# Three first passes with gate/up blocks kept on chip, passes that begin with resident blocks, and an early matmul order left to the scheduler

## Chip, cores and metric

One core of a Trainium2 chip. The metric is device microseconds of one execution. "Span" is the profiled execution's length, which is about 2 us shorter than its timed run.

Names used below: PE is the matmul engine, PEld its weight load, DVE the vector engine, ACT the scalar engine, POOL the GpSimd engine, SP the engine that issues most loads. "Idle" of an engine is a stretch's length less its busy time. Tile names in the texts: xn is the layer-normed input, hT and h2T its transposes for the projections and for gate/up, qT and kT the projected q and k, v_sb the v rows, vd their copy in memory, vsh the shifted v rows read back from it, prod and lgT the products of q and k and their sums, o_sb and oT the attention's output and its transpose, pgu and gu the gate and up results, wd and wo the loaded w_down and output weights, wmA to wmC parts of w_mod.

## The reference, cut

A transformer block on 2048 rows of 576 columns, bf16, with conditioning vectors from a small product `silu(c) @ w_mod`:

```python
h = layernorm(x) * (1 + ca) + sa
x = x + ga * attention(h, wqkv, wo)      # 32 heads of 18; each row sees 8 rows, every second one back
h = layernorm(x) * (1 + cb) + sb
x = x + gb * ((h @ w_gate) * (h @ w_up)) @ w_down     # 576 -> 4608 -> 576
```

## The kernel before

Rows are cut into chunks of 128, 128 and then 256. `period(ci)` emits the attention of chunk `ci` and the projections (q, k, v) of chunk `ci + 1`. A pass multiplies one group of chunks by all of w_gate and w_up, in nine blocks of 1.18 MB; after the last pass of a group, `down` multiplies its 512 rows by w_down. While pass i runs, a pacer emits the periods of the chunks of pass i+1 between its matmuls.

```python
SIZES = [128, 128, 256, 256, 256, 256, 256, 256, 256]
DOWN = [[[0], [1, 2]], [[3, 4]], [[5, 6]], [[7, 8]]]   # passes of 128, 384, 512, 512, 512 columns
FB = 4
GU_BUFS = 3                                             # ring of three block buffers
# ... cut
load_rows(nc.sync, wmB, w_mod[:, 3 * D:5 * D])
load_rows(nc.sync, wo, wod)                             # wod: A_wo reordered by way of a scratch copy in memory
# ... cut
for b in range(GU_BUFS):
    load_gu(0, b)                                       # blocks 0 to 2 before the first pass
# ... cut: in gate_up, after each block's matmuls
            if i == FB - 1:
                nb = b + GU_BUFS
                load_gu(pi + nb // (FT // FB), nb % (FT // FB))
                if pi == 0:
                    load_wd(b)                          # w_down is read during pass 0
# ... cut: the end of the kernel
    for _ in period(0):
        pass
    with tc.manual_schedule(engines={PE}):              # from here on PE runs in the order of emission
        passes = [(di, p) for di, d in enumerate(DOWN) for p in d]
        for pi, (di, p) in enumerate(passes):
            # ... cut
            step = Pacer(passes[pi + 1][1] if pi + 1 < len(passes) else [], total)
            step(0)
            gate_up(pi, home[p[0]][1], C, h2T[di], step)
            if last:
                down(r0, [t for q in DOWN[di] for c in q for t in x_tiles[c]], step)
            step(0, rest=True)
```

Outside `manual_schedule` the framework's scheduler chooses the order on each engine, by its own model of durations. The order then stands on the chip: in the trace of the kernel before, PE waits 2.9 us (to 123.2 us) for ACT's copy of the v rows, with gate/up matmuls behind that wait in its order.

Of the kernel before, what the change touches and what calls it, by code (L numbers as in the profile page):

```python
# [7 lines left out]
BF = mybir.dt.bfloat16  # L8
F32 = mybir.dt.float32
ALU = mybir.AluOpType  # L10
ACTF = mybir.ActivationFunctionType
# [5 lines left out]
P = 128  # L17
D = 576
DP = 640
KT = 5  # L20
H = 32
DH = 18
# [4 lines left out]
FT = FF // P  # L27
# [3 lines left out]
CM = 512  # L31
CH = 256
SIZES = [128, 128, 256, 256, 256, 256, 256, 256, 256]

DOWN = [[[0], [1, 2]], [[3, 4]], [[5, 6]], [[7, 8]]]
FB = 4
GU_BUFS = 3

AT = dict(lg0=.06, lg1=.14, lgT=.19, hT=.24, q0=.29, q1=.34, k0=.39, k1=.44, qkr=.48, v0=.52, v1=.57,
          oT=.66, wo0=.70, wo1=.74, h2T=.92)  # L40
# [3 lines left out]
def kernel(  # L44
# [37 lines left out]
    def att(shape, dt, name):  # L82
        return ps_att.tile(shape, dt, name=name, tag="att")
# [36 lines left out]
    kT = once.tile([P, KT, HALO + CH], BF, name="kT")  # L120
    v_sb = once.tile([P, D], BF, name="v_sb")
    vd = dramp.tile([HALO + S, D], BF, name="vd")
    wod = dramp.tile([D, D], BF, name="wod")

    nc.gpsimd.memset(wqk[64:, KT - 1, :], 0.0)
    nc.gpsimd.memset(wo[64:, KT - 1, :], 0.0)
# [13 lines left out]
    def load_rows(eng, dst, src):  # L140

        eng.dma_start(dst[:, 0:KT - 1, :], src[0:(KT - 1) * P, :].rearrange("(k p) n -> p k n", p=P))
        eng.dma_start(dst[0:64, KT - 1, :], src[(KT - 1) * P:D, :])
# [2 lines left out]

    setup_guard = tc.tile_pool(name="setup", bufs=1)
    sp = setup_guard.__enter__()
    c_bf = sp.tile([P, KT], BF, name="c_bf")
    nc.vector.memset(c_bf[:], 0.0)  # L150
    with nc.allow_non_contiguous_dma(reason="tiny column-layout load of c"):
        nc.sync.dma_start(c_bf[:, 0:KT - 1], c[0, 0:(KT - 1) * P].rearrange("(m p) -> p m", p=P))
        nc.sync.dma_start(c_bf[0:64, KT - 1:KT], c[0, (KT - 1) * P:D].rearrange("(m p) -> p m", p=64))

    def wm_tile():
        return sp.tile([P, KT, 2 * D], BF, name="wm", bufs=2)
# [12 lines left out]
    wmC = wm_tile()  # L169
    load_rows(nc.sync, wmC[:, :, 0:D], w_mod[:, 2 * D:3 * D])  # L170
    load_rows(nc.sync, wmC[:, :, D:2 * D], w_mod[:, 5 * D:6 * D])
    nc.sync.dma_start(wod[:, :].rearrange("(d h) n -> d h n", d=DH), A_wo.rearrange("(h d) n -> d h n", d=DH))
    wmB = wm_tile()
    load_rows(nc.sync, wmB, w_mod[:, 3 * D:5 * D])
    load_rows(nc.sync, wo, wod)

    c_f = sp.tile([P, KT], F32, name="c_f")
    nc.vector.tensor_copy(c_f[:], c_bf[:])
    e_f = sp.tile([P, KT], F32, name="e_f")
    nc.scalar.activation(e_f[:], c_f[:], ACTF.Exp, scale=-1.0)  # L180
    nc.vector.tensor_scalar_add(e_f[:], e_f[:], 1.0)
    nc.vector.reciprocal(e_f[:], e_f[:])
    sc = sp.tile([P, KT], BF, name="sc")
    nc.vector.tensor_tensor(sc[:], c_f[:], e_f[:], ALU.mult)
    sc_bc = sp.tile([P, KT, P], BF, name="sc_bc")
    nc.vector.tensor_copy(sc_bc[:], sc[:, :, None].to_broadcast([P, KT, P]))

# [29 lines left out]


    gu_blocks = {}

    def load_gu(mi, b):
        if mi >= sum(len(d) for d in DOWN):
            return
        gm = gwp.tile([P, KT - 1, 2, FB * P], BF, name="gm")
        gr = gwp.tile([P, 2, FB * 64], BF, name="gr")
        c0 = b * FB * P
        for t, wsrc in enumerate((B_w_gate, B_w_up)):
            nc.sync.dma_start(gm[:, :, t, :], wsrc[0:(KT - 1) * P, c0:c0 + FB * P].rearrange("(k p) n -> p k n", p=P))
            for half in range(2):
                nc.sync.dma_start(gr[64 * half:64 * (half + 1), t, :],  # L230
                                  wsrc[(KT - 1) * P:D, c0 + half * FB * 64:c0 + (half + 1) * FB * 64])
        gu_blocks[mi, b] = (gm, gr)

    def load_wd(b):
        n = FT * FB // FT
        nc.sync.dma_start(wd[:, b * n:(b + 1) * n, :], B_w_down[b * n * P:(b + 1) * n * P, :].rearrange("(k p) n -> p k n", p=P))

    for b in range(GU_BUFS):
        load_gu(0, b)

    def setup_mid():
        for t in range(2):
# [17 lines left out]
    def ln_rows(src):  # L260
        ST = len(src)
        stats = small.tile([P, CH // P, 2, 6], F32, name="ln_stats")
        mv = small.tile([P, CH // P, 2], F32, name="ln_mv")
        for j in range(ST):
            for hf in range(2):
                nc.vector.bn_stats(stats[:, j, hf, :], src[j][:, hf * 288:(hf + 1) * 288])  # L266
            nc.vector.bn_aggr(mv[:, j, :], stats[:, j, :, :].rearrange("p a b -> p (a b)"))
        rstd = small.tile([P, CH // P], F32, name="ln_rstd")
        nc.vector.tensor_scalar_add(rstd[:, 0:ST], mv[:, 0:ST, 1], EPS)
        nc.scalar.activation(rstd[:, 0:ST], rstd[:, 0:ST], ACTF.Ln)  # L270
        nc.scalar.activation(rstd[:, 0:ST], rstd[:, 0:ST], ACTF.Exp, scale=-0.5)
        nmr = small.tile([P, CH // P], F32, name="ln_nmr")
        nc.vector.scalar_tensor_tensor(nmr[:, 0:ST], mv[:, 0:ST, 0], -1.0, rstd[:, 0:ST], ALU.mult, ALU.mult)  # L273
        for j in range(ST):
            nc.scalar.activation(xn[:, j, 0:D], src[j][:], ACTF.Identity, bias=nmr[:, j:j + 1], scale=rstd[:, j:j + 1])  # L275
            nc.gpsimd.tensor_copy(xn[:, j, D:], xn[:, j, D - 64:D])

    def ln_cols(dst, C, vi, act_only=False):

# [161 lines left out]
    def gate_up(pi, c0, C, h2, step):  # L441

        hh = late["hh"]
        cs = slice(c0, c0 + C)
        ns = C / 2.4
        pss = {}
        for f in range(FT):
            b, i = f // FB, f % FB
            gm, gr = gu_blocks[pi, b]

            fi = (i // 2) + 2 * (i % 2)
            ps = ps_mlp.tile([P, 2, 512], F32, name="pgu", tag="mlp")
            pss[i % 2] = ps
            for t in range(2):
                for kt in range(KT - 1):
                    nc.tensor.matmul(ps[:, t, 0:C], lhsT=gm[:, kt, t, fi * P:(fi + 1) * P], rhs=h2[:, kt, cs],  # L456
                                     start=(kt == 0), stop=False, skip_group_check=True)
            if i % 2 == 0:
                step(8 * ns)
                continue  # L460
            for t in range(2):
                for hf in range(2):
                    rows = slice(64 * hf, 64 * (hf + 1))
                    nc.tensor.matmul(pss[hf][:, t, 0:C], lhsT=gr[rows, t, (i // 2) * P:(i // 2 + 1) * P],  # L464
                                     rhs=h2[rows, KT - 1, cs], start=False, stop=True, skip_group_check=True)
            with hp():
                for hf in range(2):
                    fo = b * FB + i // 2 + 2 * hf
                    gu = late["gup"].tile([P, 2, CM], BF, name="gu")
                    nc.scalar.copy(gu[:, :, 0:C], pss[hf][:, :, 0:C])  # L470
                    nc.vector.tensor_tensor(hh[:, fo, cs], gu[:, 0, 0:C], gu[:, 1, 0:C], ALU.mult)  # L471
            if i == FB - 1:
                nb = b + GU_BUFS
                load_gu(pi + nb // (FT // FB), nb % (FT // FB))
                if pi == 0:
                    load_wd(b)
            step(10 * ns)

    def down(r0, x_t, step):
        hh = late["hh"]  # L480
        for j in range(CM // P):
            acc = ps_mlp.tile([P, 2, 512], F32, name="acc", tag="mlp")
            for f in range(FT):
                for q in range(2):
                    nc.tensor.matmul(acc[:, q, 0:288], lhsT=hh[:, f, j * P:(j + 1) * P], rhs=wd[:, f, q * 288:(q + 1) * 288],  # L485
                                     start=(f == 0), stop=(f == FT - 1))
                step(240)
            with hp():
                o_t = late["outp"].tile([P, D], BF, name="y")
                nc.vector.tensor_tensor(o_t[:].rearrange("p (n d) -> p n d", n=2), acc[:, :, 0:288],  # L490
                                        gb_bc[:].rearrange("p (n d) -> p n d", n=2), ALU.mult)
                nc.vector.tensor_tensor(o_t[:], o_t[:], x_t[j][:], ALU.add)  # L492
            nc.gpsimd.dma_start(out_flat[r0 + j * P:r0 + (j + 1) * P, :], o_t[:])  # L493
# [50 lines left out]
    for _ in period(0):  # L544
        pass

    with tc.manual_schedule(engines={PE}):
        passes = [(di, p) for di, d in enumerate(DOWN) for p in d]
        for pi, (di, p) in enumerate(passes):
            last = p is DOWN[di][-1]  # L550
            C = sum(SIZES[c] for c in p)
            total = FT * 9 * C / 2.4 + (FT * CM // P * 240 if last else 0)
            step = Pacer(passes[pi + 1][1] if pi + 1 < len(passes) else [], total)
            step(0)
            gate_up(pi, home[p[0]][1], C, h2T[di], step)
            if last:
                r0 = START[DOWN[di][0][0]]
                down(r0, [t for q in DOWN[di] for c in q for t in x_tiles[c]], step)
            step(0, rest=True)


# [28 lines left out]
```

## Time and profile before

| | value |
|---|---|
| median of the first 3 runs | 656.75 us (656.70 to 659.48) |
| span of the profiled run | 655.4 us |
| PE busy | 586.0 us (89%) |
| moved by DMA | 92.38 MB |

From the page of the kernel before: busy time by engine, then 40 equal slices of the span (16.4 us each) with PE's busy share in tenths and PE's granted clock in tenths of full speed.

```profile
PE 586.0 (89%) x4405; PEld 347.6 (53%) x4449; DVE 311.5 (48%) x657; ACT 257.4 (39%) x432; POOL 62.7 (10%) x139
...
PE   3665858678999999999999999999999999999996
...
PEclk9965989779999999999999899999999999999999
```

PE is full from the eleventh digit on. The loss is in the ten before it, where the granted clock is lower at times as well.

The same in four stretches of the kernel before: set-up; to the start of the second pass; to the start of the first 512-column pass (just after the first down); the rest. Columns: stretch, its length, busy time and count of PE, PEld, DVE, ACT and POOL, granted PE clock, DMA share, GB/s.

```profile
core 0: us, PE busy (x) PEld busy (x) DVE busy (x) ACT busy (x) POOL busy (x), PEclk, DMA share, GB/s
0.00:58.46 58.46, 30.46 (x321) 23.06 (x323) 26.25 (x71) 17.82 (x48) 17.54 (x42) 0.82 0.90 290
58.46:141.02 82.56, 58.65 (x652) 42.49 (x656) 51.51 (x126) 36.09 (x90) 8.36 (x19) 0.85 0.69 217
141.02:269.21 128.19, 123.64 (x964) 77.80 (x967) 70.66 (x147) 55.94 (x97) 13.41 (x30) 0.97 0.46 142
269.21:655.40 386.19, 373.22 (x2473) 204.25 (x2504) 163.11 (x314) 147.59 (x199) 23.36 (x48) 1.00 0.33 102
```

The second line: PE is idle 82.56 - 58.65 = 23.9 us there, with DVE busy 51.5 us.

### The profile page before, as it was taken

The numbers are of one execution on the slowest core, as the hardware profiler recorded it, in microseconds if no ns is written. First come the engines' busy times: TensorE is split into PE (matmuls) and PEld (weight loads), VectorE is DVE, ScalarE is ACT, GpSimd is POOL, SyncE is SP. The second block draws the span as 40 slices with busy tenths as digits, with TensorE's granted clock in tenths as the row PEclk, the third lists the DMA queues.
The fourth block names the chain that finished last, engine by engine and source line by source line (L and its number), as shares of the span: only waits on it lengthen the run. The fifth ranks groups of instructions, "written<-read, shape, count | busy, mean of one in ns | idle before, by whom it ended". The sixth has DMA issues, their size and how long they took to land.

```text
span 655.4 us, 10904 instructions
## 1 busy us (share of the span) xinstructions
PE 586.0 (89%) x4405; PEld 347.6 (53%) x4449; DVE 311.5 (48%) x657; ACT 257.4 (39%) x432; POOL 62.7 (10%) x139
## 2 busy tenths in 40 slices
PE   3665858678999999999999999999999999999996
PEld 2453646334654677544443677454445773333575
DVE  2364738547545675376346635384447432222111
ACT  2333554245456411354475222354554023444300
POOL 4401010100010012200100011100000000000000
PEclk9965989779999999999999899999999999999999
DMA  8979784744376514143733331234645102542000
GB/s 277 321 265 324 221 269 145 259 122 131 122 226 190 146 63 138 37 145 109 261 110 118 109 101 56 81 109 135 210 146 144 56 10 81 145 145 72 1 19 19
DMA packets 81035, 92.38 MB, mean 141 GB/s; under 512 B 6601, under 2 KB 74265, under 8 KB 80985
## 3 DMA queue, kind: packets, MB, share of 16 engines
q1 hardware_dynamic: 72153, 65.73, 33.6%
q0 software_dynamic: 5952, 23.01, 9.9%
q10 hardware_dynamic: 2880, 2.95, 1.3%
q8 instruction: 35, 0.57, 0.3%
q14 instruction: 15, 0.12, 0.1%
HBM read 86.93 MB, written 5.40 MB: 141 GB/s over the span
## 4 chain that ended last, share of the span: by engine, by line
PE 67%; DVE 12%; DMA 8%; issue 6%; ACT 5%; SPq 1%; POOL 0%; POOLq 0%; DVEq 0%; ACTq 0%
PE pgu L456 32%; PE acc L485 15%; PE pgu L464 6%; PE pq L316 4%; DMA wm<-in_w_mod_dram 3%; PE lgT L375 2%; DVE vsh L409 2%; PE pw L429 2%; PE pv L332 2%; DMA gm<-in_B_w_up_dram 1%; DMA vsh<-vd 1%; DVE ln_stats L266 1%; ACT xn L275 1%; DMA wv_raw<-in_A_wqkv_dram 1%; ACT gu L470 1%
## 5 line engine op out<-in xcount | busy, mean ns | idle before, releaser
L456 PE MATMUL pgu<-h2T,gm 128*128 128x512 bf16 (+2 forms) x1409 | 276.8, 344 | 5.2 <-ACT h2T L292 2.3
L470 ACT CAST gu<-pgu 128x1024 bf16<-128x1024 f32 (+2 forms) x180 | 143.0, 844 | 163.5 <-PE pgu L464 156.4
L456 PEld LDWEIGHTS <-gm 128*128 128x128 bf16 x1440 | 129.3, 101 | 130.7 <-issue 28.4
L485 PE MATMUL acc<-wd,hh 128*128 128x288 bf16 x1152 | 146.1, 286 | 0.0
L471 DVE TENSOR_TENSOR hh<-gu 128x512 bf16<-128x512 bf16 (+2 forms) x180 | 65.2, 369 | 158.7 <-ACT gu L470 158.3
L485 PEld LDWEIGHTS <-hh 128*128 128x128 bf16 x1152 | 111.4, 98 | 29.6 <-issue 1.3
L366 DVE TENSOR_TENSOR prod<-qT,kT 128x1280 bf16<-128x1280 bf16 (+1 forms) x72 | 46.3, 686 | 22.1 <-PE lgT L375 21.9
L316 PE MATMUL pq<-hT,wqk 128*128 128x256 bf16 (+1 forms) x360 | 45.9, 280 | 10.4 <-DVE hT L290 6.7
L409 DVE TENSOR_TENSOR vsh<-vsh,attn 128x2304 bf16<-128x2304 bf16 x32 | 42.6, 1353 | 15.1 <-DMA vsh<-vd 15.0
L353 POOL DMA_DIRECT2D vsh<-vd x32 | 24.0, 751 | 266.5 <-DVE vsh L410 122.8
L464 PE MATMUL pgu<-h2T,gr 64*128 64x512 bf16 (+2 forms) x360 | 47.4, 343 | 0.9
L316 PEld LDWEIGHTS <-wqk 128*128 128x128 bf16 x360 | 34.3, 107 | 21.0 <-issue 15.4
L490 DVE TENSOR_TENSOR y<-acc,gb_bc 128x576 bf16<-128x576 f32 x16 | 12.1, 754 | 50.2 <-PE acc L485 50.2
L266 DVE BATCH_NORM_STATS2 ln_stats<-x_t 128x6 f32<-128x288 bf16 x64 | 25.6, 438 | 6.1 <-DMA x_t<-in_A_x_dram 5.6
L275 ACT ACTIVATE xn<-x_t,ln_nmr,ln_rstd 128x576 bf16<-128x576 bf16 x32 | 27.0, 863 | 2.2 <-DVE ln_nmr L273 1.7
L464 PEld LDWEIGHTS <-gr 64*128 64x128 bf16 x360 | 10.3, 95 | 31.0 <-issue 27.6
L493 POOL DMA_DIRECT2D out_dram<-y x16 | 8.8, 549 | 168.1 <-DVE y L492 158.1
L429 PE MATMUL pw<-wo,oT 128*128 128x512 bf16 x74 | 23.6, 413 | 0.6 <-ACT oT L422 0.6
L285 PE MATMUL ln_pA<-ident,xn 128*128 128x128 bf16 x128 | 11.0, 228 | 12.2 <-ACT xn L275 12.2
L410 DVE TENSOR_TENSOR vsh<-vsh 128x2304 bf16<-128x2304 bf16 x16 | 21.7, 1353 | 0.2
L332 PE MATMUL pv<-wv,hT 128*128 128x512 bf16 x74 | 21.2, 380 | 0.4 <-ACT kT L318 0.2
L336 ACT CAST v_sb<-pv 128x512 bf16<-128x512 f32 x16 | 9.4, 589 | 30.3 <-PE pvr L334 17.6
(98 smaller groups left out, 394.9 us busy)
## 6 DMA issues: line engine op xcount, KB each, us to landing
gm<-in_B_w_gate_dram SPq DMA_DIRECT2D x45, 512.0 KB, 3.8
gm<-in_B_w_up_dram SPq DMA_DIRECT2D x45, 512.0 KB, 4.9
vsh<-vd POOLq DMA_DIRECT2D x32, 576.0 KB, 5.5
wd<-in_B_w_down_dram SPq DMA_DIRECT2D x9, 576.0 KB, 9.9
gr<-in_B_w_gate_dram SPq DMA_DIRECT2D x90, 32.0 KB, 3.6
gr<-in_B_w_up_dram SPq DMA_DIRECT2D x90, 32.0 KB, 4.2
wm<-in_w_mod_dram SPq DMA_DIRECT2D x2, 1152.0 KB, 10.0
vd<-v_sb ACTq DMA_DIRECT2D x16, 144.0 KB, 3.9
```

Of the source, the lines that this page charges most:

```text
L266: nc.vector.bn_stats(stats[:, j, hf, :], src[j][:, hf * 288:(hf + 1) * 288])
L275: nc.scalar.activation(xn[:, j, 0:D], src[j][:], ACTF.Identity, bias=nmr[:, j:j + 1], scale=rstd[:, j:j + 1])
L316: nc.tensor.matmul(pq[:, gi, 0:C], lhsT=wqk[:, kt, w0:w0 + P], rhs=hT[:, kt, 0:C], start=(kt == 0), stop=(kt == KT - 1))
L332: nc.tensor.matmul(pv[:], lhsT=hT[:, kt, j * P:(j + 1) * P], rhs=wv[:, kt, 0:512], start=(kt == 0), stop=(kt == KT - 1))
L366: nc.vector.tensor_tensor(prod[:, 0:nm, 0:C], qT[:, 0:nm, 0:C], kT[:, 0:nm, off:off + C], ALU.mult)
L409: nc.vector.tensor_tensor(vsh[:], vsh[:], attn[:, j, ws, None, :].to_broadcast([P, WG, DH, H]), ALU.mult)
L429: nc.tensor.matmul(pw[:], lhsT=oT[:, m, j * P:(j + 1) * P], rhs=wo[:, m, 0:512], start=(m == 0), stop=(m == KT - 1))
L456: nc.tensor.matmul(ps[:, t, 0:C], lhsT=gm[:, kt, t, fi * P:(fi + 1) * P], rhs=h2[:, kt, cs], start=(kt == 0), stop=False, skip_group_check ...
L464: nc.tensor.matmul(pss[hf][:, t, 0:C], lhsT=gr[rows, t, (i // 2) * P:(i // 2 + 1) * P], rhs=h2[rows, KT - 1, cs], start=False, stop=True, ...
L470: nc.scalar.copy(gu[:, :, 0:C], pss[hf][:, :, 0:C])
L471: nc.vector.tensor_tensor(hh[:, fo, cs], gu[:, 0, 0:C], gu[:, 1, 0:C], ALU.mult)
L485: nc.tensor.matmul(acc[:, q, 0:288], lhsT=hh[:, f, j * P:(j + 1) * P], rhs=wd[:, f, q * 288:(q + 1) * 288], start=(f == 0), stop=(f == FT ...
```

## The change

The intent: more matmul work where PE has none, and freedom to use it. The first 512 rows go through gate/up in three passes (128, 128, 256) instead of two (128, 384). A third pass would read all nine blocks again, so four of them stay on chip for these passes, in the memory of w_down, which is read only when pass 2 has used them. Each pass begins with blocks that the pass before left in the ring. PE's order in these three passes is the scheduler's. Three set-up edits come along: c is loaded as rows and transposed on PE, wo is loaded by eighteen small copies without the scratch copy, and a 64-column copy moves from POOL to ACT.

```diff
-DOWN = [[[0], [1, 2]], [[3, 4]], [[5, 6]], [[7, 8]]]
+DOWN = [[[0], [1], [2]], [[3, 4]], [[5, 6]], [[7, 8]]]
+AUTO = 3
+ORDER = [[0, 1, 2, 3, 4, 5, 6, 7, 8], [6, 7, 8, 5, 4, 3, 2, 1, 0], [2, 3, 4, 5, 8, 1, 0, 6, 7],
+         [0, 6, 7, 1, 2, 3, 4, 5, 8], [4, 5, 8, 0, 1, 2, 3, 6, 7], [3, 6, 7, 0, 1, 2, 4, 5, 8]]
+KEPT = [2, 3, 4, 5]
 ...
-    c_bf = sp.tile([P, KT], BF, name="c_bf")            (c in columns)
+    c_row = sp.tile([KT, P], BF, name="c_row")          (c in rows; silu on rows; transposed on PE)
 ...
-    nc.sync.dma_start(wod[...], A_wo...)                 (ahead of wmB)
     wmB = wm_tile()
     load_rows(nc.sync, wmB, w_mod[:, 3 * D:5 * D])
-    load_rows(nc.sync, wo, wod)
+    for d in range(DH):
+        r0 = d % 4 * H
+        nc.sync.dma_start(wo[r0:r0 + H, d // 4, :], A_wo.rearrange("(h d) n -> d h n", d=DH)[d])
 ...
+    def block_done(pi, b):
+        if pi == 2 and b in KEPT:
+            k = KEPT.index(b)
+            load_wd(k * WDB, (k + 1) * WDB)
+        for n in range(len(loads)):
+            if last_use[n] == (pi, b) and n + GU_BUFS == state["next"]:
+                load_next()
+    for b in ORDER[0]:
+        if b in KEPT:
+            load_gu(b, KEPT.index(b))                     (into the memory of w_down)
+        elif state["next"] < GU_BUFS:
+            load_next()
+    load_wd(len(KEPT) * WDB, FT)
 ...
-            nc.gpsimd.tensor_copy(xn[:, j, D:], xn[:, j, D - 64:D])
+            nc.scalar.activation(xn[:, j, D:], src[j][:, D - 64:], ...)
 ...
+    for pi in range(AUTO):
+        run_pass(pi)                                      (PE order by the scheduler)
     with tc.manual_schedule(engines={PE}):
-        for pi, (di, p) in enumerate(passes):
+        for pi in range(AUTO, len(passes)):
+            run_pass(pi)
```

More of the change, by code (lines that the diff above doesn't have):

```diff
@@ L33 @@
 SIZES = [128, 128, 256, 256, 256, 256, 256, 256, 256]
-DOWN = [[[0], [1, 2]], [[3, 4]], [[5, 6]], [[7, 8]]]
+DOWN = [[[0], [1], [2]], [[3, 4]], [[5, 6]], [[7, 8]]]
 FB = 4
+AUTO = 3
 GU_BUFS = 3
+NB = FT // FB
+ORDER = [[0, 1, 2, 3, 4, 5, 6, 7, 8], [6, 7, 8, 5, 4, 3, 2, 1, 0], [2, 3, 4, 5, 8, 1, 0, 6, 7],
+         [0, 6, 7, 1, 2, 3, 4, 5, 8], [4, 5, 8, 0, 1, 2, 3, 6, 7], [3, 6, 7, 0, 1, 2, 4, 5, 8]]
+KEPT = [2, 3, 4, 5]
 AT = dict(lg0=.06, lg1=.14, lgT=.19, hT=.24, q0=.29, q1=.34, k0=.39, k1=.44, qkr=.48, v0=.52, v1=.57,
@@ L122 @@
     vd = dramp.tile([HALO + S, D], BF, name="vd")
-    wod = dramp.tile([D, D], BF, name="wod")
     nc.gpsimd.memset(wqk[64:, KT - 1, :], 0.0)
@@ L148 @@
     sp = setup_guard.__enter__()
-    c_bf = sp.tile([P, KT], BF, name="c_bf")
-    nc.vector.memset(c_bf[:], 0.0)
-    with nc.allow_non_contiguous_dma(reason="tiny column-layout load of c"):
-        nc.sync.dma_start(c_bf[:, 0:KT - 1], c[0, 0:(KT - 1) * P].rearrange("(m p) -> p m", p=P))
-        nc.sync.dma_start(c_bf[0:64, KT - 1:KT], c[0, (KT - 1) * P:D].rearrange("(m p) -> p m", p=64))
+    c_row = sp.tile([KT, P], BF, name="c_row")
+    nc.vector.memset(c_row[:], 0.0)
+    nc.sync.dma_start(c_row[0:KT - 1, :], c[0, 0:(KT - 1) * P].rearrange("(m p) -> m p", p=P))
+    nc.sync.dma_start(c_row[KT - 1:KT, 0:64], c[0:1, (KT - 1) * P:D])
     def wm_tile():
@@ L171 @@
     load_rows(nc.sync, wmC[:, :, D:2 * D], w_mod[:, 5 * D:6 * D])
-    nc.sync.dma_start(wod[:, :].rearrange("(d h) n -> d h n", d=DH), A_wo.rearrange("(h d) n -> d h n", d=DH))
     wmB = wm_tile()
     load_rows(nc.sync, wmB, w_mod[:, 3 * D:5 * D])
-    load_rows(nc.sync, wo, wod)
-    c_f = sp.tile([P, KT], F32, name="c_f")
-    nc.vector.tensor_copy(c_f[:], c_bf[:])
-    e_f = sp.tile([P, KT], F32, name="e_f")
+    for d in range(DH):
+        r0 = d % 4 * H
+        nc.sync.dma_start(wo[r0:r0 + H, d // 4, :], A_wo.rearrange("(h d) n -> d h n", d=DH)[d])
+    c_f = sp.tile([KT, P], F32, name="c_f")
+    nc.vector.tensor_copy(c_f[:], c_row[:])
+    e_f = sp.tile([KT, P], F32, name="e_f")
     nc.scalar.activation(e_f[:], c_f[:], ACTF.Exp, scale=-1.0)
@@ L182 @@
     nc.vector.reciprocal(e_f[:], e_f[:])
+    sc_row = sp.tile([KT, P], BF, name="sc_row")
+    nc.vector.tensor_tensor(sc_row[:], c_f[:], e_f[:], ALU.mult)
+    pc = att([P, KT], BF, "pc")
+    nc.tensor.transpose(pc[:], sc_row[:], ident[0:KT, 0:KT])
     sc = sp.tile([P, KT], BF, name="sc")
-    nc.vector.tensor_tensor(sc[:], c_f[:], e_f[:], ALU.mult)
+    nc.vector.tensor_copy(sc[:], pc[:])
     sc_bc = sp.tile([P, KT, P], BF, name="sc_bc")
@@ L219, with load_gu @@
     gu_blocks = {}
-    def load_gu(mi, b):
-        if mi >= sum(len(d) for d in DOWN):
-            return
-        gm = gwp.tile([P, KT - 1, 2, FB * P], BF, name="gm")
-        gr = gwp.tile([P, 2, FB * 64], BF, name="gr")
+    wd_flat = wd[:].rearrange("p f d -> p (f d)")
+    GM, GR = (KT - 1) * 2 * FB * P, 2 * FB * 64
+    def load_gu(b, kept=None):
+        if kept is None:
+            gm = gwp.tile([P, KT - 1, 2, FB * P], BF, name="gm")
+            gr = gwp.tile([P, 2, FB * 64], BF, name="gr")
+        else:
+            o = kept * (GM + GR)
+            gm = wd_flat[:, o:o + GM].rearrange("p (k t n) -> p k t n", k=KT - 1, t=2)
+            gr = wd_flat[:, o + GM:o + GM + GR].rearrange("p (t n) -> p t n", t=2)
         c0 = b * FB * P
@@ L231, in load_gu, with load_next, load_wd @@
                                   wsrc[(KT - 1) * P:D, c0 + half * FB * 64:c0 + (half + 1) * FB * 64])
-        gu_blocks[mi, b] = (gm, gr)
-    def load_wd(b):
-        n = FT * FB // FT
-        nc.sync.dma_start(wd[:, b * n:(b + 1) * n, :], B_w_down[b * n * P:(b + 1) * n * P, :].rearrange("(k p) n -> p k n", p=P))
-    for b in range(GU_BUFS):
-        load_gu(0, b)
+        gu_blocks[b] = (gm, gr)
+    loads, last_use, ring = [], [], {}
+    for pi, order in enumerate(ORDER):
+        for b in order:
+            if b in KEPT and pi < 3:
+                continue
+            if b not in ring:
+                if len(loads) >= GU_BUFS:
+                    del ring[loads[len(loads) - GU_BUFS]]
+                ring[b] = len(loads)
+                loads.append(b)
+                last_use.append(None)
+            last_use[ring[b]] = (pi, b)
+    WDB = (GM + GR) // D
+    state = dict(next=0)
+    def load_next():
+        if state["next"] < len(loads):
+            load_gu(loads[state["next"]])
+            state["next"] += 1
+    def load_wd(f0, f1):
+        nc.sync.dma_start(wd[:, f0:f1, :], B_w_down[f0 * P:f1 * P, :].rearrange("(k p) n -> p k n", p=P))
+    def block_done(pi, b):
[7 more added lines that the diff above has]
+        if b in KEPT:
+            load_gu(b, KEPT.index(b))
+        elif state["next"] < GU_BUFS:
+            load_next()
+    load_wd(len(KEPT) * WDB, FT)
     def setup_mid():
@@ L275, in ln_rows @@
             nc.scalar.activation(xn[:, j, 0:D], src[j][:], ACTF.Identity, bias=nmr[:, j:j + 1], scale=rstd[:, j:j + 1])
-            nc.gpsimd.tensor_copy(xn[:, j, D:], xn[:, j, D - 64:D])
+            nc.scalar.activation(xn[:, j, D:], src[j][:, D - 64:], ACTF.Identity, bias=nmr[:, j:j + 1], scale=rstd[:, j:j + 1])
     def ln_cols(dst, C, vi, act_only=False):
@@ L446, in gate_up @@
         pss = {}
-        for f in range(FT):
-            b, i = f // FB, f % FB
-            gm, gr = gu_blocks[pi, b]
+        for n in range(FT):
+            b, i = ORDER[pi][n // FB], n % FB
+            gm, gr = gu_blocks[b]
             fi = (i // 2) + 2 * (i % 2)
@@ L472, in gate_up @@
             if i == FB - 1:
-                nb = b + GU_BUFS
-                load_gu(pi + nb // (FT // FB), nb % (FT // FB))
-                if pi == 0:
-                    load_wd(b)
+                block_done(pi, b)
             step(10 * ns)
@@ L545, with run_pass @@
         pass
-    with tc.manual_schedule(engines={PE}):
-        passes = [(di, p) for di, d in enumerate(DOWN) for p in d]
-        for pi, (di, p) in enumerate(passes):
-            last = p is DOWN[di][-1]
-            C = sum(SIZES[c] for c in p)
-            total = FT * 9 * C / 2.4 + (FT * CM // P * 240 if last else 0)
-            step = Pacer(passes[pi + 1][1] if pi + 1 < len(passes) else [], total)
-            step(0)
-            gate_up(pi, home[p[0]][1], C, h2T[di], step)
-            if last:
-                r0 = START[DOWN[di][0][0]]
-                down(r0, [t for q in DOWN[di] for c in q for t in x_tiles[c]], step)
-            step(0, rest=True)
+    passes = [(di, p) for di, d in enumerate(DOWN) for p in d]
+    def run_pass(pi):
+        di, p = passes[pi]
+        last = p is DOWN[di][-1]
+        C = sum(SIZES[c] for c in p)
+        total = FT * 9 * C / 2.4 + (FT * CM // P * 240 if last else 0)
+        step = Pacer(passes[pi + 1][1] if pi + 1 < len(passes) else [], total)
+        step(0)
+        gate_up(pi, home[p[0]][1], C, h2T[di], step)
+        if last:
+            r0 = START[DOWN[di][0][0]]
+            down(r0, [t for q in DOWN[di] for c in q for t in x_tiles[c]], step)
+        step(0, rest=True)
+    for pi in range(AUTO):
+        run_pass(pi)
+    with tc.manual_schedule(engines={PE}):
+        for pi in range(AUTO, len(passes)):
+            run_pass(pi)
 _INS = ['A_x', 'A_wqkv', 'A_wo', 'B_x', 'B_w_gate', 'B_w_up', 'B_w_down', 'c', 'w_mod']
```

## The prediction

> **What bounds the kernel now.** By the windows of the trace TensorE (PE) is nearly full from 141 us to 614 us (461.4 of 473.5 us). The loss is early. From 0 to 58.5 us (set-up, chunk 0) PE is busy 30.5 us with DMA at 90%. From 58.5 to 141.0 us (first pass, 128 columns, over the attention of chunks 1 and 2) it is busy only 58.7 of 82.5 us, at a granted clock of 0.85. The chain of waits there runs through ACT, DVE and DMA: softmax, the vsh products (1.35 us each), vsh<-vd (5.1 us), v_sb waiting for vd<-v_sb (4.2 us), layer norm, h2T; the gate/up matmuls that could fill it stand at fixed places in PE's order. The Trainium skill ("TensorE: Matmul & The Clock Gate", Part 1) says that an idle PE is clocked down; the 0.85 here against 1.00 from 501 us on agrees.
>
> **What the change does.**
> 1. Passes 128+128+256 replace 128+384. Columns, and so PE work, are equal (eight gate/up matmuls: 0.45 us at 128 columns, 1.3 at 384). But chunk 1's gate/up, about 360 x 55 ns = 18 to 20 us, now falls under chunk 2's attention, where PE sat idle 13.7 of 43.5 us. Four blocks kept in wd's place spare reloads: 31 block loads instead of 45 (1.18 MB each, 16.5 MB less).
> 2. Early PE order by the scheduler: independent gate/up work fills waits that the fixed order leaves (24 us idle from 58 to 141 us).
> 3. Set-up: the wod round trip (648 KB written and read) leaves the queue ahead of wmB, on which PE waits 3.3 us at 30.5 us; against it, eighteen small issues on SP, about 0.5 us each. c comes in rows, and the 64-column copy moves from POOL to ACT (32 x about 0.25 us): a hop less in each layer norm.
> 4. Seven blocks (8.3 MB) come before pass 0 in place of three blocks and seven down loads (7.6 MB): DMA load before 58 us about equal. "DMAs issued from the SP, ACT and POOL queues all run on the same 16 DMA engines" (Trainium Kernel Development and Optimization, Key Constraints), so after 58 us vsh and vd should land sooner with fewer block loads (DMA was 87% busy from 58 to 97 us).
>
> **Sum (estimates from these durations).** Set-up 3 to 5 us; 58 to 141 us: idle 24 us falls to about 8, and a better clock gives 3 to 5: about 20; stage to the end of the first down (141 to 270 us, clock 0.96, 4.6 us idle): 2 to 4; later passes 0 to 2. Together about 28 us: **629 us, range 612 to 646**. Chances: faster 0.86, same 0.11, slower 0.03.
>
> **What would show it.** First down ending near 240 us instead of 270; PE idle before that point down by some 20 us; granted clock there over 0.9; later passes as long as before (142, 130, 109 us with their down); first gate/up at 53 to 56 us; DMA bytes near 76 MB instead of 92.
>
> **What would make it wrong.** The scheduler orders PE by its model; if that model has DMA or ACT too fast, PE, which runs in order, stands before a load while other work is ready. The attention chain of chunks 1 and 2 (39 and 43 us) may stay as long, so the gain comes only from moving 18 us. Down loads now wait for pass 2. Eighteen wo issues could delay the first blocks.

The quotation in its point 4 leaves out the names that the page puts in brackets behind SP, ACT and POOL. The 55 ns a matmul are the trace's eight in 0.45 us (56 ns).

## More of the kernel before

The top of the table of PE's waits in the kernel before, from 57 to 142 us (waiting line, what it waited for, total us, times, longest us):

```profile
PE ln_pA L285 <- ACT xn L275: 7.4, 3, 3.9
PE oT_pA L421 <- ACT v_sb L336: 6.1, 2, 3.2
PE pvr L334 <- DVE kT L326: 2.5, 2, 1.3
```

All are steps of the attention of chunks 1 and 2: a layer norm on ACT, the v rows waiting for their copy out, a transposed output. The gate/up matmuls of pass 0 could fill such waits, but each stands at a fixed place in PE's order.

## The result

| | before | after |
|---|---|---|
| median of 4 runs each | 657.20 us (656.70 to 659.48) | 639.62 us (636.37 to 639.84) |
| ratio to before | 1 | 0.9714, 95% interval 0.9675 to 0.9753 |
| span | 655.4 us | 637.8 us |
| moved by DMA | 92.38 MB | 75.23 MB |

Executions over 1.5% slower than the fastest of the same kernel are left out of the means. A ratio here and below is the mean time of one kernel's runs over that of the other's of the same rounds, so it is not quite the ratio of the medians. Medians of different sessions differ by 1 to 3 us for the same kernel (before: 656.2 to 658.6 us), so kernels of different sessions are compared by their ratios.

The page of the kernel after, the same lines:

```profile
PE 587.7 (92%) x4766; PEld 362.8 (57%) x4810; DVE 316.6 (50%) x694; ACT 270.9 (42%) x500; POOL 53.1 (8%) x107
...
PE   1876999989999999999998999999999999999996
...
PEclk9965899999989999999999999999999999999999
```

PE is now nearly full from the fifth digit on. The same four stretches of the kernel after (the second pass to start is now the 256-column one, the third):

```profile
core 0: us, PE busy (x) PEld busy (x) DVE busy (x) ACT busy (x) POOL busy (x), PEclk, DMA share, GB/s
0.00:57.31 57.31, 31.17 (x321) 23.23 (x324) 27.34 (x72) 18.13 (x50) 14.54 (x38) 0.82 0.80 255
57.31:142.36 85.05, 78.14 (x1012) 58.70 (x1016) 57.77 (x164) 50.42 (x136) 6.71 (x13) 0.94 0.56 176
142.36:252.98 110.62, 106.50 (x963) 77.17 (x967) 68.46 (x146) 50.13 (x104) 11.37 (x20) 0.97 0.38 121
252.98:637.80 384.82, 371.86 (x2473) 203.70 (x2504) 163.06 (x315) 152.21 (x213) 20.52 (x36) 1.00 0.28 84
```

The whole sum can be read from these eight lines:

| stretch | before us (PE idle) | after us (PE idle) |
|---|---|---|
| set-up | 58.5 (28.0) | 57.3 (26.1) |
| to the pass that completes the first 512 rows | 82.6 (23.9) | 85.1 (6.9) |
| that pass and the first down | 128.2 (4.6) | 110.6 (4.1) |
| the rest | 386.2 (13.0) | 384.8 (13.0) |

The second stretch grew by 2.5 us although it holds one more pass, and the third shrank by 17.6 us as that work left it. Over the two together PE's idle time fell by 28.5 - 11.0 = 17.4 us and its busy time rose by 2.4 us. With 1.2 us from the set-up and 1.4 us from the rest this is the whole 17.6 us of span. The top of the table of PE's waits in the kernel after, 57 to 142 us, and from further down the only one on a block load:

```profile
PE pgu L504 <- ACT gu L518: 1.4, 2, 0.8
PE ln_pA L333 <- ACT xn L323: 1.4, 2, 0.9
PE lgT L423 <- ACT h2T L340: 0.7, 1, 0.7
...
PE pgu L504 <- DMA gm<-in_B_w_up_dram: 0.6, 1, 0.6
```

The waits on ACT for the layer norm and on v_sb, 7.4 and 6.1 us before, are 1.4 us and none here.

### The profile page after: what moved, and what is told of

It is laid out like the page before. It is cut to its first block, busy times and chain, and to the rows that moved or that the text cites. A ratio compares the mean times of both kernels' runs of the same rounds, so it can differ in the third digit from the quotient of the medians.

```text
span 637.8 us, 11591 instructions
## 1 busy us (share of the span) xinstructions
PE 587.7 (92%) x4766; PEld 362.8 (57%) x4810; DVE 316.6 (50%) x694; ACT 270.9 (42%) x500; POOL 53.1 (8%) x107
## 2 busy tenths in 40 slices
DMA packets 60782, 75.23 MB, mean 118 GB/s; under 512 B 4842, under 2 KB 54010, under 8 KB 60730
## 4 chain that ended last, share of the span: by engine, by line
PE 56%; DVE 10%; issue 6%; ACT 4%; DMA 2%; POOL 0%; SPq 0%; POOLq 0%; DVEq 0%; ACTq 0%
PE pgu L504 28%; PE acc L530 15%; PE pgu L512 5%; PE pq L364 2%; DVE vsh L457 2%; PE lgT L423 2%; ACT gu L518 2%; DMA vsh<-vd 1%; PE pv L380 1%; PE pw L477 1%; ACT xn L323 1%; DVE ln_stats L314 1%; DVE ssum L446 1%; DVE vsh L458 1%; DMA gm<-in_B_w_up_dram 1%
## 5 line engine op out<-in xcount | busy, mean ns | idle before, releaser
L504 PE MATMUL pgu<-h2T,gm 128*128 128x512 bf16 (+2 forms) x1313 | 243.2, 333 | 3.6 <-ACT gu L518 1.1
L518 ACT CAST gu<-pgu 128x1024 bf16<-128x1024 f32 (+2 forms) x216 | 147.1, 730 | 158.1 <-PE pgu L512 155.3
L504 PEld LDWEIGHTS <-gm 128*128 128x128 bf16 x1344 | 116.5, 100 | 111.6 <-issue 19.2
L519 DVE TENSOR_TENSOR hh<-gu 128x512 bf16<-128x512 bf16 (+2 forms) x216 | 70.3, 333 | 152.8 <-ACT gu L518 152.0
L414 DVE TENSOR_TENSOR prod<-qT,kT 128x1280 bf16<-128x1280 bf16 (+1 forms) x72 | 46.1, 685 | 17.8 <-PE lgT L423 17.6
L512 PE MATMUL pgu<-h2T,gr 64*128 64x512 bf16 (+2 forms) x336 | 44.2, 335 | 0.9
L504 PE MATMUL pgu<-h2T,wd 128*128 128x128 bf16 (+1 forms) x384 | 37.4, 240 | 1.5 <-ACT gu L518 0.8
L504 PEld LDWEIGHTS <-wd 128*128 128x128 bf16 x384 | 27.3, 98 | 7.4 <-issue 4.2
L477 PE MATMUL pw<-wo,oT 128*128 128x512 bf16 x74 | 22.3, 396 | 0.7 <-ACT oT L470 0.6
L380 PE MATMUL pv<-wv,hT 128*128 128x512 bf16 x74 | 21.1, 381 | 0.5 <-DVE kT L374 0.2
```

The lines of the kernel that those rows point to most:

```text
L414: nc.vector.tensor_tensor(prod[:, 0:nm, 0:C], qT[:, 0:nm, 0:C], kT[:, 0:nm, off:off + C], ALU.mult)
L477: nc.tensor.matmul(pw[:], lhsT=oT[:, m, j * P:(j + 1) * P], rhs=wo[:, m, 0:512], start=(m == 0), stop=(m == KT - 1))
L504: nc.tensor.matmul(ps[:, t, 0:C], lhsT=gm[:, kt, t, fi * P:(fi + 1) * P], rhs=h2[:, kt, cs], start=(kt == 0), stop=False, skip_group_check ...
L512: nc.tensor.matmul(pss[hf][:, t, 0:C], lhsT=gr[rows, t, (i // 2) * P:(i // 2 + 1) * P], rhs=h2[rows, KT - 1, cs], start=False, stop=True, ...
L518: nc.scalar.copy(gu[:, :, 0:C], pss[hf][:, :, 0:C])
L519: nc.vector.tensor_tensor(hh[:, fo, cs], gu[:, 0, 0:C], gu[:, 1, 0:C], ALU.mult)
```

## The experiments

All runs gave results within the reference's tolerance.

### Which part earned it: passes or scheduler

First the changed kernel with PE's order fixed in every pass:

```diff
-AUTO = 3
+AUTO = 0
```

> The changed kernel with PE's order fixed by the program for all six passes (no pass left to the scheduler). Theory W (work): the gain came from the 18 to 20 us of chunk 1's gate/up that now lie under chunk 2's attention, not from the scheduler; then this kernel loses at most 5 us to the changed one (under 645 us). Theory S (scheduler): letting independent matmuls pass those that wait is what took the 17 us of idle PE away; then it loses 8 us or more (over 648 us), with PE waits on ACT and DVE back in the stretch to 142 us.

Measured: 648.11 us, ratio 0.9876 (0.9834 to 0.9918); it has the set-up edits too. Then the kernel before with its old passes, PE's order left to the scheduler in the first two (set-up edits not included):

```diff
-    with tc.manual_schedule(engines={PE}):
-        for pi, (di, p) in enumerate(passes): ...
+    for pi in range(2):
+        run_pass(pi)
+    with tc.manual_schedule(engines={PE}):
+        for pi in range(2, len(passes)):
+            run_pass(pi)
```

> The kernel before, passes of 128 and 384, with only the PE order of these two passes left to the scheduler. Theory W: within 4 us of before (653 to 661), as pass 0's 20 us of gate/up only run earlier and PE then lacks work. Theory S: 8 us or more faster (under 649).

Measured: 648.30 us, ratio 0.9862 (0.9823 to 0.9900). The middle two stretches of each, first of the fixed order with the new passes:

```profile
55.79:146.56 90.77, 76.62 (x1016) 58.24 (x1016) 58.68 (x162) 49.91 (x134) 7.24 (x13) 0.93 0.55 172
146.56:261.06 114.50, 106.80 (x968) 77.61 (x967) 68.51 (x147) 49.72 (x105) 11.73 (x20) 0.96 0.36 117
```

and of the old passes with the scheduler:

```profile
59.46:138.19 78.73, 59.40 (x656) 42.00 (x656) 51.32 (x128) 36.25 (x92) 9.50 (x20) 0.80 0.75 239
138.19:261.73 123.54, 122.06 (x967) 76.74 (x967) 70.50 (x146) 55.17 (x95) 13.19 (x29) 0.99 0.43 137
```

By the thresholds set beforehand theory S held in both runs, though narrowly (648.11 against "over 648", 648.30 against "under 649"), and theory W in neither; with the fixed order PE's waits on ACT and DVE add up to 13.1 us in the stretch to 146.6 us. But the thresholds left out that both parts may give something, and the idle time shows that they do. In the stretch to the completing pass PE's idle time is 23.9 us before, 90.77 - 76.62 = 14.2 us with the new passes alone, 78.73 - 59.40 = 19.3 us with the scheduler alone and 6.9 us with both; the scheduler alone also takes 3 of the 4.6 us that follow. In time, each part alone is worth about 1.3% (with an interval wholly under 1), and the product of the two ratios, 0.974, is close to the 0.971 of both. Within the noise the two add up; neither does the other's work.

### Are the kept blocks needed

The changed kernel with no kept blocks; the orders are chosen anew so that a pass still begins with the three blocks in the ring, and w_down is read during pass 0 as before:

```diff
-KEPT = [2, 3, 4, 5]
+KEPT = []
+        if pi == 0:
+            load_wd(b * FB, (b + 1) * FB)
-    load_wd(len(KEPT) * WDB, FT)
```

> The changed kernel with passes of 128, 128 and 256 and the scheduler, but no blocks kept on chip: every pass reads its blocks through the three ring buffers (39 block loads, 3 spared by starting with those on chip), down weights read during pass 0 as before. If keeping the blocks is what makes a third pass affordable: PE waits for block loads appear and the time is 5 to 15 us over the changed kernel (645 to 655). If DMA had room (it was 38 to 66% busy from 68 to 142 us), within 3 us of it.

Measured: 654.82 us, ratio 0.9970 (0.9927 to 1.0013). Almost the whole gain is lost. Its middle two stretches:

```profile
57.31:157.56 100.25, 83.75 (x1016) 61.30 (x1016) 58.84 (x162) 50.05 (x133) 6.68 (x13) 0.91 0.76 246
157.56:267.75 110.19, 105.48 (x970) 76.82 (x967) 68.75 (x148) 50.95 (x107) 12.03 (x20) 0.98 0.38 122
```

The loss is in the first of them, 100.3 us instead of 85.1, at a DMA share of 0.76 instead of 0.56. PE is idle there for 100.25 - 83.75 = 16.5 us instead of 6.9. The table of PE's waits in this stretch (us in total, times, longest) shows loads of w_up on top:

```profile
PE pgu L505 <- DMA gm<-in_B_w_up_dram: 5.1, 2, 3.5
PE ln_pA L334 <- ACT xn L324: 2.9, 2, 1.6
...
PE pgu L513 <- DMA gr<-in_B_w_up_dram: 1.5, 1, 1.5
```

That is 5.1 + 1.5 = 6.6 us, and 0.6 us in the kernel after. Waits on loads are thus shown as the larger part of the 9.6 us of added idle time, though not of the whole 15 us: PE was also busy 83.75 us instead of 78.14, at a granted clock of 0.91 instead of 0.94. The order differs too. On PE of this kernel the transposes of chunk 2's attention output come late:

```profile
138.41 0.62 PE L470 MATMUL oT_pA<-ident,o_sb 128*128 128x128 bf16 x8
```

and on DVE of the same kernel:

```profile
125.10 0.46 DVE L463 TENSOR_TENSOR o_sb<-vsh 128x576 bf16<-128x576 bf16 x1
```

The output o_sb is ready at 125.6 us, but its transposes start at 138.4 us. PE was not standing still between them: it ran gate/up matmuls and projections of chunk 3, which its order placed first. In the kernel after, the same two steps, PE and then DVE:

```profile
127.97 0.56 PE L469 MATMUL oT_pA<-ident,o_sb 128*128 128x128 bf16 x7
```

```profile
127.47 0.45 DVE L462 TENSOR_TENSOR o_sb<-vsh 128x576 bf16<-128x576 bf16 x1
```

There PE goes on with the transposes at 128.0 us, as soon as o_sb is done. So without blocks kept on chip the third pass doesn't pay. Waits on loads are part of the reason; how the rest divides between the other order and the clock stays open. The edit also moves the reading of w_down back under the first pass, so the loads that PE waited behind are not the blocks' second reading alone.

### The set-up edits

> The changed kernel with the three set-up edits undone (c by columns, wo by way of the scratch copy, the 64-column copy on POOL). By the traces set-up ends 1.15 us earlier with them, so 0 to 3 us slower than the changed kernel (639 to 643). If the eighteen wo issues (18.3 us on SP) delay the blocks and that costs more than it gives, this kernel is faster than the changed one.

Edit: all three set-up edits undone. Measured: 636.74 us (633.76 to 639.63), ratio 0.9676 (0.9627 to 0.9724): not slower than the kernel after, and its set-up is 2.1 us longer (59.4 us). So the set-up edits earn nothing that the times show. To split them, c alone was put back into columns, together with an unaltered run of the changed kernel as a yardstick:

> The changed kernel unaltered, as the yardstick for the other three on the same chip: 636 to 641 us.

Measured: 636.94 us (634.56 to 640.38), ratio 0.9705 (0.9672 to 0.9738), span 638.7 us, the 256-column pass starting at 145.2 us; in the first trace of the same kernel it was 142.4. Two traces of one kernel thus differ by 2.8 us at this point, at granted clocks of 0.94 and 0.91 in the stretch before it, and smaller differences between single traces say little.

```diff
-    c_row = sp.tile([KT, P], BF, name="c_row")
+    c_bf = sp.tile([P, KT], BF, name="c_bf")            (and the silu on [P, KT], no transpose)
```

> The changed kernel with only the loading of c undone (columns again). In the changed kernel's trace the first matmuls on w_mod start at 13.3 us instead of 10.7, because c in rows needs longer vector operations (reciprocal 0.94 us instead of 0.19) and a transpose. If set-up is bound by that chain, the first gate/up starts about 2 us earlier (near 55.3 us) and the time falls by 1 to 3 us. If the landing of wmB, the vsh loads or DVE bind next, it falls by less than 1 us.

Measured: 638.23 us, ratio 0.9718 (0.9688 to 0.9747). In the trace the set-up is 55.1 us, 2.3 to 2.7 shorter than in the changed kernel's two traces, as expected; the median is no better. The third pass starts at 140.6 us there, 1.8 us before that of the kernel after. A shorter set-up is real in the trace and doesn't show in the times, but with four and six runs these don't resolve the lower part of the 1 to 3 us expected. The last pair below looks at it again.

In the trace of the kernel after, the eighteen wo copies hold SP from 18.6 to 36.9 us, and the first block waits behind them. From 26 to 30 us DMA (the share is the number before the last) stands nearly idle in the kernel after

```profile
26.00:30.00 4.00, 3.34 (x19) 1.45 (x20) 1.07 (x4) 1.37 (x5) 0.76 (x1) 1.00 0.17 47
```

while in the kernel before it was full:

```profile
26.00:30.00 4.00, 1.16 (x9) 0.36 (x6) 0.00 (x0) 0.70 (x2) 0.00 (x0) 1.00 1.04 348
```

The Trainium skill ("DMA: Bandwidth & Descriptors", Issuing engines are not separate DMA queues) calls issue time "usually small relative to the DMA itself". The trace agrees for these copies: 0.42 us to issue one, and a median of 5.0 us (the last number) from issue to landing.

```profile
wo<-in_A_wo_dram SPq DMA_DIRECT2D x18, 36.0 KB, 5.0
```

More than half of the 18.3 us went into SP's waits between the copies, one of them 7.6 us long (21.1 to 28.7 us), around the time in which DMA stood nearly idle; what SP waited for there is not settled. The first block is issued at 37.1 us instead of 25.1. It costs little here, as PE takes up the first block only at 57 us and waits 0.6 us for blocks in the whole stretch.

### Is the clock the limit

From 57.3 to 68.3 us PE of the kernel after is busy 10.98 of 10.99 us at a granted clock of 0.54. The edit fills the idle time before it with matmuls that are thrown away:

```diff
+        if ci == 0:
+            for i in range(14):
+                nc.tensor.matmul(ps[:, 0, :], lhsT=oT[:, i % 4, 0:P], rhs=wo[:, i % 4, 0:512], start=True, stop=True)
         ln_rows(x_t)
```

> The changed kernel with fourteen matmuls of 512 columns into an unused accumulator (result thrown away) after chunk 0's output projection, where PE is idle 4.8 us. Theory C (clock): from 57.3 to 68.3 us PE is busy all the time at a granted clock of 0.54, so about 5 us are lost to the clock; kept busy, the clock is near 1.0 there and the first two passes end 3 to 5 us earlier (635 us or less). Theory D (loads): the blocks, whose issue the eighteen wo copies hold up until 37 to 68 us, are the next limit; then PE waits on block loads appear in pass 0 and the gain is under 2 us. Theory A (attention): the chain of chunks 1 and 2 sets the end of the stretch; then less than 2 us as well, with PE waits on ACT or DVE.

Measured: 637.17 us (631.87 to 640.13), ratio 0.9685 (0.9646 to 0.9724), not told apart from the yardstick's 0.9705. Two microseconds of the kernel after (the clock is the third number from the right), of the kernel with the extra matmuls, and of the yardstick, which is the kernel after once more, without extra matmuls:

```profile
62.00:64.00 2.00, 2.00 (x18) 1.27 (x16) 0.68 (x3) 0.75 (x3) 0.00 (x0) 0.50 0.96 295
62.00:64.00 2.00, 2.00 (x36) 1.58 (x38) 1.10 (x6) 0.74 (x2) 0.54 (x2) 1.00 0.98 292
62.00:64.00 2.00, 2.00 (x32) 1.56 (x28) 0.90 (x4) 1.21 (x4) 0.00 (x0) 1.00 0.90 263
```

Beside the first trace the edit seems to have worked on the clock: 1.00 from 62 us instead of from 68. But the yardstick has 1.00 there without it. And two microseconds after the start of the first pass the clock was 0.50 with the extra matmuls too; the same stretch of that kernel and of the yardstick:

```profile
58.00:60.00 2.00, 2.00 (x26) 1.41 (x23) 1.04 (x3) 1.68 (x3) 0.26 (x1) 0.50 1.13 322
58.00:60.00 2.00, 2.00 (x23) 1.11 (x23) 0.62 (x3) 2.00 (x5) 0.00 (x0) 0.50 1.05 296
```

The fourteen matmuls had filled 3.2 us of the gap of 4.8 us. So the edit gave the gate/up matmuls about 1 us more at full clock than the yardstick had, and theory C was hardly put to the test. The 256-column pass started at 144.1 us, 1.0 us earlier than in the yardstick and 1.7 us later than in the first trace, which is less than these two traces of one kernel differ by. The means of six runs each are 636.8 and 637.5 us. Theory C is neither confirmed nor refuted. PE's waits on block loads were 1.7 us in all from 50 to 145 us, so theory D has little to show.

The record gives a reason not to drop the clock. Of the ten runs of the changed kernel, the three with a mean granted clock of 0.980 to 0.983 took 634.6 to 636.4 us, the two with 0.972 and 0.973 took 636.7 and 637.2, and the five with 0.967 to 0.971 took 639.5 to 640.4. That is a relation; whether the clock makes the time, or more idle time makes the clock, isn't shown. Both traces of this kernel are of runs with a low clock (0.970 and 0.968), and a few us between single traces of two kernels can be a difference of clock.

### Is it the attention chain

Two edits tried to shorten the chain directly. The first gives the attention's matmuls priority over gate/up in the scheduler's passes:

```diff
-                            nc.tensor.matmul(lgT[...], lhsT=ind[...], rhs=rhs, ...)
+                with hp():  nc.tensor.matmul(lgT[...], lhsT=ind[...], rhs=rhs, ...)      (also lg, oT, pw)
```

> The changed kernel with high priority, in the scheduler's passes, for the matmuls and transposes of the attention (lgT, lg, oT, pw). Theory A: the end of the second pass (142.4 and 145.2 us in two traces) is set by the attention chain of chunks 1 and 2, which the scheduler lengthens by putting gate/up matmuls between its steps (lgT of chunk 2 takes 9 to 14 us instead of 5 in the kernel before); then lgT of chunk 2 takes about 5 us, the 256-column pass starts at 140 us or sooner, and the time falls by 2 to 5 us. Rival W: PE work fills that stretch (78 us busy of 85); then the order does not matter and the pass starts within 1.5 us of 142 to 145.

Measured: 641.28 us, ratio 0.9753 (0.9715 to 0.9791). The matmuls of lgT for chunk 2 still took from 96.5 to 106.2 us, so the edit did not do what it was made for, and the pass started at 146.3 us. PE waited 2.2 us for a block and 4.8 us at the end for a layer norm. The second moves the products of gate and up from DVE to POOL in the first two passes:

```diff
-                    nc.vector.tensor_tensor(hh[:, fo, cs], ...)
+                    (nc.gpsimd if pi < 2 else nc.vector).tensor_tensor(hh[:, fo, cs], ...)
```

> The changed kernel with the products of gate and up (hh, 72 of 0.22 us on DVE in the first two passes, 15 us) done on POOL in those two passes. If DVE, 58 of 85 us busy between 57 and 142 us, lengthens the attention chain of chunks 1 and 2, the 256-column pass starts 2 to 6 us earlier. If the chain is latency and PE order, no change (within 1.5 us). If POOL is slow (over 0.5 us each) and holds up the buffers, later.

Measured: 642.47 us, ratio 0.9762 (0.9734 to 0.9789), the pass starting at 145.8 us. DVE was busy 48.1 us instead of 57.8, with no gain. A product took 0.60 us on POOL against 0.22 on DVE, and the vsh products on DVE took 1.43 us instead of 1.35 beside it. But ACT's copies of gu waited 8.3 us for POOL's products, and PE once 3.3 us for such a copy, so the edit put a wait of its own in. Theory A is thus neither confirmed nor refuted: taking DVE work away did not help in this form, and the other edit did not shorten the chain it meant to shorten.

### All passes by the scheduler, and a better version

```diff
-AUTO = 3
+AUTO = 6
```

> The changed kernel with all six passes ordered by the scheduler. If the scheduler's order is better everywhere, the 512-column passes (384.8 us with 13 us of idle PE) lose up to 5 us of it. If it helps only where PE lacks work, within 2 us of the changed kernel; if it delays attention work behind gate/up matmuls in later passes, slower.

Measured: 635.52 us (632.61 to 636.92), ratio 0.9670 (0.9639 to 0.9700). The last stretch is 382.2 us instead of 384.8, and it is 382.3 and 381.8 in the two kernels that follow, so this gain of about 2.5 us repeats. The last two runs put it together with set-up edits undone: c in columns alone,

> The changed kernel with the two edits that looked best put together: c by columns (set-up 2.5 us shorter in its trace) and all six passes ordered by the scheduler (later passes 382.2 instead of 384.8 us). If both hold and add up, the ratio to the kernel before is 0.963 to 0.966 (the changed kernel: 0.9705); if the set-up gain is given back as the times of the c edit alone suggest, it stays at 0.967.

and all three undone:

> The same with all three set-up edits undone (wo by the scratch copy and the 64-column copy on POOL as well). If set-up time passes through to the end, this is 3 to 5 us slower than its partner, as its first gate/up starts near 59.4 us instead of 55. If not, because early blocks or a shorter attention chain later make up for it, within 1.5 us of it.

Measured: 634.08 us, ratio 0.9638 (0.9611 to 0.9665), and 635.90 us, ratio 0.9656 (0.9629 to 0.9682). The first lies in the range expected if both gains add up (0.963 to 0.966), and its interval just excludes 0.967. The second is 1.8 us slower, between the 1.5 and the 3 us that were to tell, so this pair of times decides nothing about the set-up. The first of the two is the best version found: its interval lies just under the one of the changed kernel (0.9672 to 0.9738, of another session). The second stretch of it, whose ends can be read from its first column:

```profile
54.14:143.65 89.51, 80.78 (x1012) 60.10 (x1016) 57.95 (x164) 50.48 (x136) 6.69 (x13) 0.90 0.57 181
```

and of its partner:

```profile
61.04:146.14 85.10, 78.44 (x1013) 59.40 (x1016) 58.17 (x164) 47.35 (x128) 9.04 (x20) 0.92 0.49 154
```

The set-ups differ by 6.9 us, the starts of the 256-column pass by 2.5, the spans by 1.3 (635.1 and 636.4), the medians by 1.8. In this pair of traces most of what the set-up gains is given back before the third pass. In the edit of c alone it was not: of 2.3 us, 1.8 were left there. How much of a shorter set-up arrives is not settled.

## Why the prediction was right, and where it was off

The range (612 to 646) held the measured 639.6 us, and "faster", given 0.86, came true (by more than 2%). The range was 34 us wide, so that it held says little about the sum. The gain was 17.6 us where about 28 had been summed. Against the sum: PE's idle time in the second stretch fell by 17.0 us (16 expected) and in the third by 0.4 (2 to 4), set-up and the rest gave 1.2 and 1.4 (3 to 5, and 0 to 2), and PE's busy time, of which a better clock was to save 3 to 5, rose by 2.4. Point by point:

- **Idle PE in the first passes: right.** "Idle 24 us falls to about 8": it fell from 23.9 to 6.9 us. The two causes named, work moved under chunk 2's attention and a free order, were each shown to hold, about half of the gain each.
- **"Columns, and so PE work, are equal": the term that was left out.** Narrow matmuls cost more per column. The timeline of PE below times two column tiles (sixteen full matmuls and four half ones) from the start of the first to the start of what follows; the granted clock is 1.00 around all three. The kernel before, 384 columns: 158.49 - 155.36 = 3.13 us.

```profile
155.36 2.76 PE L456 MATMUL pgu<-h2T,gm 128*128 128x384 bf16 x16
158.06 0.50 PE L464 MATMUL pgu<-h2T,gr 64*128 64x384 bf16 x4
158.49 0.29 PE L285 MATMUL ln_pA<-ident,xn 128*128 128x128 bf16 x2
```

  The kernel after, 128 and 256 columns: 136.00 - 134.72 = 1.28 us and 152.05 - 149.88 = 2.17 us.

```profile
134.72 1.13 PE L504 MATMUL pgu<-h2T,gm 128*128 128x128 bf16 x16
135.78 0.28 PE L512 MATMUL pgu<-h2T,gr 64*128 64x128 bf16 x4
136.00 1.13 PE L504 MATMUL pgu<-h2T,gm 128*128 128x128 bf16 x16
...
149.88 1.92 PE L504 MATMUL pgu<-h2T,wd 128*128 128x256 bf16 x16
151.73 0.39 PE L512 MATMUL pgu<-h2T,wd 64*128 64x256 bf16 x4
152.05 0.29 PE L423 MATMUL lgT<-prod,ind 128*32 128x256 bf16 x2
```

  There are eighteen such pairs in a pass, so the 128- and 256-column passes cost (1.28 + 2.17 - 3.13) x 18 = 5.8 us more PE time than one of 384. This is an estimate; where PE alternates between kinds of work a 128-column pair takes about 1.20 us, which makes it 4.3. The prediction had counted these matmuls at their best pace. PE's busy time rose by 2.4 us only; the likely reason is that less of it ran at a low clock, as estimated below.
- **"Set-up 3 to 5 us": mis-sized.** It was 1.15 us. PE no longer waits for wmB, as predicted, but c in rows starts the first w_mod matmuls at 13.3 us instead of 10.7. Beyond that, no experiment showed a gain in set-up clearly in the times. The copy on ACT was costed at 0.25 us and took 0.44.
- **"A better clock gives 3 to 5": plausible, not shown as a gain of its own.** The clock of the second stretch rose from 0.85 to 0.94, over 0.9 as foreseen (0.91 in the yardstick's trace). An estimate from the traces: PE's busy time in each microsecond times one less its granted clock, summed over the second and third stretch, is 13.8 us before, 8.3 after and 9.2 in the yardstick. So some 5 us less of matmul time were lost to the clock, about what the narrower matmuls cost: two terms that nearly cancel, of which the sum had counted only the first. The run meant to test the clock alone hardly changed it. A busy PE is not a fast one: from 57 to 68 us it was full at 0.54. The Trainium skill ("Trainium Kernel Development and Optimization", Performance Expectations) calls matmul busy time "a bad metric" for the distance from the peak, for another reason, that matmuls are pipelined; the half clock is one more that this trace shows.
- **What should have shown it.** The end of the first down was put "near 240 us"; it came at 253 (before: 269). The first gate/up was to start at 53 to 56 us; it started at 57.3. DMA bytes near 76 MB: 75.2. Later passes as before: 384.8 against 386.2 us.
- **The rival given, that the attention of chunks 1 and 2 may take as long as before** "so the gain comes only from moving 18 us", is what the first trace looks like: the pass after it starts at 142.4 us, 141.0 before. The scheduler's half of the gain shows there as a third pass's worth of work in nearly the same time.

What stays open: what sets the start of the 256-column pass. In the ten kernels with three passes and kept blocks it lay between 140.6 (c in columns) and 146.6 us (fixed order). Neither the spare matmuls, nor less DVE work, nor priority for the attention matmuls moved it below the 142.4 us of the first trace, but none of these edits tested its theory cleanly, and a set-up 6.9 us shorter moved it by 2.5. A chain through attention, PE order and loads is a plausible reason, argued and not shown, and the clock stays a rival.

## What to carry to other kernels

Where an engine lacks work in one stretch and is full in the next, cut the work finer so that a piece of it becomes ready earlier, and pay for the second reading of its operands with memory that isn't needed yet; without that memory the same cut gained almost nothing here. A scheduler helps where independent work can pass a waiting chain, but its order stands on the chip: in the kernel without kept blocks PE stood up to 3.5 us before a load that landed late. Check where a saving arrives: in one pair of traces a set-up 6.9 us shorter was worth 2.5 us at the third pass. And compare an experiment with an unaltered run of its own session: here the first trace alone would have shown an effect on the clock that the yardstick has without the edit.

## What the Trainium skill lacked or had wrong

- "DMA: Bandwidth & Descriptors", Issuing engines are not separate DMA queues: nothing wrong here, issue time was small beside the DMA (0.42 against 5.0 us for a copy of 36 KB). What we found on no page is what can hold SP between copies: eighteen of them took 18.3 us, more than half of it waiting, with DMA at a share of 0.17 from 26 to 30 us. What SP waited for is not settled.
- "TensorE: Matmul & The Clock Gate", Back-to-back issue gap: about 81 ns a matmul at 128 columns in a stream of weight loads and matmuls. Here sixteen 128-column matmuls, with weight loads of their own (50 matmuls and 47 loads from 134 to 137 us), took 1.06 us at a granted clock of 1.00, or 66 ns each.
- The same page, Part 1: an idle PE is clocked down. In the kernel before PE was busy 0.53 us of the four from 120 to 124 us, and the clock fell from 1.00 to 0.50. How long the half clock lasts under full work varied between two traces of the kernel after: from 57.3 to about 67 us in the first, from 57.8 to about 61 us in the yardstick's.
- "GPSIMD Engine Reference", 8. Key points: POOL shares its memory interfaces with DVE where a DVE instruction has two inputs there, and DVE is called about twice as fast for elementwise work. This case showed 2.7 times: a product of 128x128 bf16 took 0.60 us on POOL (whose spans the profile gives only roughly) and 0.22 on DVE. Beside 72 such products on POOL, DVE products of 128x2304 took 1.43 us on average instead of 1.35, which agrees with the first statement without proving its cause.
